# One more resident weight granule for one stream slot less, in a recurrent-memory attention kernel

## The chip, the cores and the metric

The kernel runs on one core of a Trainium2 chip. The metric is the device time of one execution in microseconds (us).

## The reference, cut to what matters

```python
for s in range(n_seg):                                   # 64 segments of 32 rows, one after the other
    h = jnp.concatenate([mem, xs], axis=1)               # 8 memory rows + 32 rows of the segment
    q, k, v = (einsum('btd,dhe->bhte', h, W) for W in (Wq, Wk, Wv))   # D=1024, 32 heads of 128
    p = softmax(mask(q @ k.T * scale))
    o = einsum('bhte,hed->btd', p @ v, Wo)
    mem = o[:, :M, :]                                    # the next segment needs this
    outs.append(o[:, M:, :])
# + a 2-token expert layer (w_gate, w_up, w_down) and two residual sums at the end
```

The memory rows make the segments sequential. Every segment needs all of Wq, Wk, Wv and Wo: 4 x 8 MB in bf16. That is 64 pieces of 512 KB, called granules, and they do not all fit beside each other in the core's memory.

Of the kernel before, what the change touches and what calls it, by code (L numbers as in the profile page):

```python
# [14 lines left out]
PSUM = bass.MemoryType.PSUM  # L15
DRAM = bass.MemoryType.DRAM

N_RES = 42
N_SLOT = 6

HELD = (18, 27, 36)
NEG = -30000.0

PHASES = [(0, 0), (1, 0), (0, 1), (1, 1), (2, 0), (2, 1)]
# [3 lines left out]
def kernel(  # L28
# [42 lines left out]
    NG = 64  # L71
    n_str = NG - N_RES
    streamed = set(((2 * i + 1) * NG) // (2 * n_str) for i in range(n_str))
    assert all(g in streamed and g < 48 for g in HELD)

    def granule_dram(g):
        if g < 48:
            p, kc = divmod(g, KC)
            mat, half = PHASES[p]
            return Wqkv[mat][kc * P:(kc + 1) * P, 2048 * half:2048 * (half + 1)]  # L80
        w = g - 48
        return Wo2[2 * w * P:(2 * w + 2) * P, :].rearrange("(hh e) d -> e hh d", hh=2)

    def granule_out(t, g):
        return t[:, :] if g < 48 else t.rearrange("p (hh d) -> p hh d", hh=2)
# [3 lines left out]
    dram = ctx.enter_context(tc.tile_pool(name="dram", bufs=1, space=DRAM))  # L89
    wstream = ctx.enter_context(tc.tile_pool(name="wstream", bufs=N_SLOT))  # L90
    one = ctx.enter_context(tc.tile_pool(name="one", bufs=1, reuse_waits="tile"))
# [117 lines left out]
    def fetch():  # L209

        while flow:
            what = flow.pop(0)
            if what[0] == "w" and what[1] not in streamed:
                g = what[1]
                pool = wres
                if g >= 48:
                    if late["pool"] is None:
                        pc.close()
                        late["pool"] = lc.enter_context(tc.tile_pool(name="wlate", bufs=1, reuse_waits="tile"))
                    pool = late["pool"]  # L220
                t = res_tiles[g] = pool.tile([P, 2048], BF16, name=f"wres{g}", tag=f"wres{g}")
                nc.sync.dma_start(out=granule_out(t, g), in_=granule_dram(g))
                continue
            t = wstream.tile([P, 2048], BF16, tag="g", name="g")
            if what[0] == "w" and what[1] in held:
                nc.sync.dma_start(out=t[:, 0:1024], in_=granule_dram(what[1])[:, 0:1024])
                nc.scalar.copy(out=t[:, 1024:2048], in_=held[what[1]][:, :].bitcast(BF16))  # L227
            elif what[0] == "w" and what[1] in wo_in:
                nc.sync.dma_start(out=t[:, :], in_=wo_d[what[1]][:, :])
            elif what[0] == "w":  # L230
                nc.sync.dma_start(out=granule_out(t, what[1]), in_=granule_dram(what[1]))
            elif what[0] == "gu":
                _, w, kc, fh = what
                nc.sync.dma_start(out=t[:, 0:FH], in_=(B_w_gate, B_w_up)[w][kc * P:(kc + 1) * P, FH * fh:FH * (fh + 1)])
            elif what[0] == "dn":
                nc.sync.dma_start(out=t.rearrange("p (a d) -> p a d", a=2),
                                  in_=B_w_down[2 * what[1] * P:(2 * what[1] + 2) * P, :].rearrange("(a p) d -> p a d", a=2))
            queued.append((what, t))
            return
# [6 lines left out]
    lc = ExitStack()  # L246
    for _ in range(N_SLOT):
        fetch()
# [93 lines left out]
    def used(g):  # L342
        if g in streamed:
            fetch()
# [65 lines left out]
    def left_pass(L, kc, Gv):  # L410

        for jq in range(4):
            nc.tensor.matmul(L["ps"][32 * jq:32 * jq + 32, :], lhsT=cur["stl"][:, kc, :],  # L413
                             rhs=Gv[:, 512 * jq:512 * (jq + 1)], start=(not L["had"]), stop=(len(L["had"]) == KC - 1),
                             tile_position=(0, 32 * jq))
        L["had"].append(kc)

    def left_bank():
        return {"ps": psL.tile([P, 512], F32, tag="accl", name="PSl"), "had": []}

    begun = {}
    for s in range(NSEG):
# [183 lines left out]
        for p, (mat, half) in enumerate(PHASES):  # L606
# [3 lines left out]
            lag, behind = 2 if j == 0 else 0, []  # L610
            for kc in range(KC):
                g = 8 * p + kc
                Gv = granule(g)
                for jq in range(4):
                    nc.tensor.matmul(PSm[32 * jq:32 * jq + 32, :], lhsT=ST[:, kc, :], rhs=Gv[:, 512 * jq:512 * (jq + 1)],  # L615
                                     start=(kc == 0), stop=(kc == KC - 1), tile_position=(0, 32 * jq))
                if s == 0 and g in HELD:
                    held[g] = psC.tile([P, 512], U32, tag=f"c{HELD.index(g)}", name="HELD")
                    nc.vector.tensor_scalar(out=held[g][:, :], in0=Gv[:, 1024:2048].bitcast(U32), scalar1=0, scalar2=None,
# [55 lines left out]
        n_wl, behind = 0, []  # L675

        def project_left(w, Gv, WL=WL if j == 3 else None, lhs=lhs_left):

            nonlocal n_wl
            for hs in range(2):  # L680
                for a in range(2):
                    q0 = 64 * hs + 32 * a
                    nc.tensor.matmul(WL[q0:q0 + 32, :], lhsT=lhs(2 * w + hs),  # L683
                                     rhs=Gv[:, D * hs + 512 * a:D * hs + 512 * (a + 1)], start=(n_wl == 0), stop=False,
                                     tile_position=(0, q0), skip_group_check=True)
            n_wl += 1
# [29 lines left out]
        nl = left_of(s + 1) if s + 1 < NSEG else {}  # L716
        if j == 3:
            fill = [lambda w=w, Gv=Gv: project_left(w, Gv) for w, Gv in behind[:4]]
            spots = [(0, 1), (0, 2), (0, 3), (0, 5), (0, 7), (1, 1)]
            todo += [(pk, lambda w=w, Gv=Gv, go=project_left: go(w, Gv)) for pk, (w, Gv) in zip(spots, behind[4:])]  # L720
            assert len(behind) == 10
        elif j == 1 or j == 2:
            for mat in nl:
                begun[mat] = left_bank()
                fill = [lambda kc=kc, g=8 * mat + kc, L=begun[mat]: left_pass(L, kc, res_tiles[g])
                        for kc in range(KC) if 8 * mat + kc not in streamed]
# [40 lines left out]
    for w in range(2):  # L767
        for fh in range(2):
            GU[w, fh] = psA.tile([P, 512], F32, tag="acc", name="GU") if w == 0 else \
                psC.tile([P, 512], F32, tag=f"c{fh}", name="GU")  # L770
        for kc in range(KC):
            for fh in range(2):
                Gt = take("gu", w, kc, fh)

                for q in range(4):
                    nb = 4 if q < 2 else 3
                    nc.tensor.matmul(GU[w, fh][32 * q:32 * q + 32, 0:nb * P], lhsT=XSP[:, kc, :],
                                     rhs=Gt.rearrange("p (b q c) -> p q b c", q=4, c=P)[:, q, 0:nb, :],
                                     start=(kc == 0), stop=(kc == KC - 1), tile_position=(0, 32 * q))
                fetch()  # L780
                n += 1
                if n in (6, 14):
                    todo[-2 + (6, 14).index(n)][1]()
# [71 lines left out]
```

## The kernel before: the parts that the change touches

42 granules stay resident; the other 22 are loaded again in each segment through a ring of six slots. A slot and a resident granule are the same size, and 42 + 6 = 48 of them are all that fits beside the kernel's other tiles. Three streamed granules are special: half of each is held in PSUM (the matrix engine's result memory), so that only the other 256 KB are loaded. These are the "held halves".

```python
N_RES = 42
N_SLOT = 6
HELD = (18, 27, 36)
...
n_str = NG - N_RES
streamed = set(((2 * i + 1) * NG) // (2 * n_str) for i in range(n_str))
...
wstream = ctx.enter_context(tc.tile_pool(name="wstream", bufs=N_SLOT))
...
t = wstream.tile([P, 2048], BF16, tag="g", name="g")     # waits for the slot to be released
if what[0] == "w" and what[1] in held:                    # half of it is kept in PSUM
    nc.sync.dma_start(out=t[:, 0:1024], in_=granule_dram(what[1])[:, 0:1024])
    nc.scalar.copy(out=t[:, 1024:2048], in_=held[what[1]][:, :].bitcast(BF16))
elif what[0] == "w" and what[1] in wo_in:                 # Wo copied once into contiguous scratch
    nc.sync.dma_start(out=t[:, :], in_=wo_d[what[1]][:, :])
elif what[0] == "w":
    nc.sync.dma_start(out=granule_out(t, what[1]), in_=granule_dram(what[1]))
...
lag, behind = 2 if j == 0 else 0, []                      # j = s % 4
for kc in range(KC):                                      # 6 phases of 8 granules: Q, K, Q, K, V, V
    Gv = granule(g)
    for jq in range(4):
        nc.tensor.matmul(PSm[32 * jq:32 * jq + 32, :], lhsT=ST[:, kc, :], rhs=Gv[:, 512 * jq:512 * (jq + 1)], ...)
    ...                                                   # some segments: a "left pass", the same granule once more
    used(g)                                               # issues the next load, which waits for a free slot
...
for w in range(16):                                       # output projection: granules 48 to 63
    project(WO, w, Gv, lhs_main, w == 15)
    used(48 + w)
```

Phases, the softmax and the projection differ a little by j = s % 4, the "remainder" below: the left passes (rows that four segments share) fall in remainders 2, 3 and 0, and the projection of those rows in remainder 3 and the start of 0.

## Time and profile before

| | before |
|---|---|
| median of all 36 runs, us | 2049 (medians of the five sets: 2046 to 2050) |
| bytes moved by DMA | 771.7 MB |
| mean period of segments 4 to 59 | 29.6 us |
| bytes a segment | 11.26 MB |

A segment's period is taken from one start of the transposes that put the memory rows into the stationary tile (L317 in the kernel before) to the next. The lines that the argument rests on are shown and read in the prediction. In these lines PE is the matrix engine (PEld its weight loads), DVE, ACT and POOL are the other engines, and SP issues the weight loads; tile g is a stream slot and tile wres a resident granule. Landing is the moment at which a load is known to have arrived; a slot's hold is the time from there to the next issue into it. Where a number below is called a tally, it was worked out from the trace's records of single packets, issues and landings, not printed by a view.

### The profile page before, as it was taken

Reading aid. Unit: us, or ns where it says so; the run is one execution under the profiler, and the core shown is the slowest. Engines: PE = TensorE matmul, PEld = TensorE weight load, DVE = VectorE, ACT = ScalarE, POOL = GpSimd, SP = SyncE. Lnnn points to the kernel's source line nnn. Section 1 sums busy time; section 2 is a strip of 40 time slices with the busy share of each in tenths; the row PEclk is TensorE's granted clock in tenths of the full one; section 3 lists DMA queues with packets and bytes.
Section 4 is the critical chain, followed back from the end, with each engine's and each line's share of the span. In section 5 each row is a group of like instructions: output and inputs, shape, how many; then the busy total and the mean of one; then the engine's idle time right before and its main releaser. Section 6 shows DMA issues by size and latency. Waiting matters only on the chain.

```text
span 2053.8 us, 80700 instructions
## 1 busy us (share of the span) xinstructions
PE 1723.0 (84%) x35178; PEld 863.7 (42%) x35178; DVE 760.2 (37%) x2360; ACT 717.9 (35%) x1754; POOL 525.5 (26%) x1004
## 2 busy tenths in 40 slices
PE   2578888888888888898988988898898888888776
PEld 1234444444444444444444444444444444444331
DVE  5523333333343333334333433343333333333420
ACT  3623333333333333333333333333333333333320
POOL 4422222222222222222231322223222222222110
PEclk8689999999999999999999999999999999999986
DMA  9999999999999999999999999999999999999998
GB/s 358 334 375 388 375 401 362 385 380 378 382 380 387 391 383 354 366 387 376 395 391 383 378 374 383 372 379 382 391 374 367 388 379 375 380 391 371 357 345 332
DMA packets 248230, 771.73 MB, mean 376 GB/s; under 512 B 37042, under 2 KB 42354, under 8 KB 247876
## 3 DMA queue, kind: packets, MB, share of 16 engines
q1 hardware_dynamic: 221188, 732.79, 93.8%
q0 software_dynamic: 23872, 29.19, 4.1%
q8 instruction: 275, 4.51, 0.8%
q10 hardware_dynamic: 2816, 4.59, 0.6%
q14 instruction: 79, 0.65, 0.1%
HBM read 753.82 MB, written 15.74 MB: 375 GB/s over the span
## 4 chain that ended last, share of the span: by engine, by line
DMA 56%; PE 35%; DVE 3%; ACT 2%; issue 2%; POOL 1%; ACTq 0%; DVEq 0%; SPq 0%; POOLq 0%
PE PSm L615 19%; DMA g<-wo_d 18%; DMA g<-in_A_Wv_dram 13%; DMA g<-in_A_Wq_dram 12%; PE PSl L413 5%; PE OA L664 3%; PE PTq L453 2%; DMA out_dram<-OB 2%; DMA g<-in_A_Wk_dram 2%; DMA g<-in_A_Wo_dram 1%; DMA QKL<-qkl_d 1%; PE WL L683 1%; DMA qkl_d<-QS 1%; DMA wres<-in_A_Wo_dram 1%; DMA g<-in_B_w_gate_dram 1%
## 5 line engine op out<-in xcount | busy, mean ns | idle before, releaser
L615 PE MATMUL PSm<-wres,ST 128*32 128x512 bf16 x8192 | 751.9, 392 | 5.7 <-DVE ST L318 5.1
L615 PE MATMUL PSm<-g,ST 128*32 128x512 bf16 x4096 | 419.0, 392 | 78.8 <-DMA g<-in_A_Wv_dram 38.5
L615 PEld LDWEIGHTS <-ST 128*32 128x32 bf16 x12288 | 300.0, 96 | 409.5 <-issue 175.2
L664 PEld LDWEIGHTS <-OT 128*32 128x32 bf16 x8192 | 218.0, 98 | 169.3 <-issue 146.7
L227 ACT COPY g<-HELD 128x1024 bf16<-128x1024 bf16 x189 | 191.4, 1013 | 199.2 <-PE PSm L615 117.3
L634 ACT CAST XB<-PSm 128x512 bf16<-128x512 f32 x256 | 149.9, 586 | 282.5 <-PE PSm L615 281.9
L664 PE MATMUL OA<-wres,OT 128*32 128x256 bf16 x5120 | 234.8, 280 | 14.1 <-issue 8.7
L664 PE MATMUL OA<-g,OT 128*32 128x256 bf16 x3072 | 160.2, 280 | 94.0 <-DMA g<-wo_d 79.7
L413 PE MATMUL PSl<-wres,STL 128*32 128x512 bf16 x2048 | 181.2, 389 | 13.8 <-DVE XBl L638 13.2
L561 ACT CAST OT<-OA 128x128 bf16<-128x128 f32 x256 | 67.9, 265 | 256.1 <-PE OP L555 254.1
L349 POOL DMA_DIRECT2D QKL<-qkl_d x126 | 91.8, 729 | 227.7 <-PE SPS L497 89.8
L710 POOL DMA_DIRECT2D out_dram<-OB x256 | 129.5, 513 | 54.2 <-DVE OB L706 33.7
L485 POOL COPY KT<-QKL 128x128 bf16<-128x128 bf16 x128 | 37.6, 293 | 403.4 <-PE OA L664 300.5
L561 DVE CAST OT<-OP 128x128 bf16<-128x128 f32 x128 | 37.3, 291 | 252.5 <-PE OP L555 252.5
L502 DVE TENSOR_REDUCE NM<-SPS 128x8 f32<-128x320 f32 x128 | 62.9, 491 | 170.2 <-PE SPS L497 170.2
L413 PEld LDWEIGHTS <-STL 128*32 128x32 bf16 x3072 | 83.4, 98 | 88.2 <-issue 36.4
L453 PE MATMUL PTq<-IDENT,XB 128*128 128x128 bf16 x1024 | 102.9, 224 | 20.2 <-ACT XB L634 18.8
L646 ACT CAST VM<-PSm 128x512 bf16<-128x512 f32 x128 | 77.4, 604 | 116.5 <-PE PSm L615 109.0
L413 PE MATMUL PSl<-g,STL 128*32 128x512 bf16 x1024 | 102.6, 388 | 11.5 <-DVE XBl L638 8.7
L453 PEld LDWEIGHTS <-XB 128*128 128x128 bf16 x1024 | 58.8, 98 | 124.6 <-ACT XB L634 69.2
L473 POOL DMA_DIRECT2D qkl_d<-QS x64 | 36.5, 570 | 275.5 <-ACT QS L469 259.7
L706 DVE CAST OB<-OA 128x128 bf16<-128x128 f32 x64 | 18.6, 291 | 228.5 <-ACT OB L705 175.8
(143 smaller groups left out, 2334.3 us busy)
## 6 DMA issues: line engine op xcount, KB each, us to landing
g<-wo_d SPq DMA_DIRECT2D x363, 512.0 KB, 7.1
g<-in_A_Wq_dram SPq DMA_DIRECT2D x321, 512.0 KB, 7.8
g<-in_A_Wk_dram SPq DMA_DIRECT2D x257, 512.0 KB, 6.6
g<-in_A_Wv_dram SPq DMA_DIRECT2D x257, 512.0 KB, 6.8
g<-in_A_Wq_dram SPq DMA_DIRECT2D x63, 256.0 KB, 5.7
g<-in_A_Wk_dram SPq DMA_DIRECT2D x63, 256.0 KB, 5.7
g<-in_A_Wv_dram SPq DMA_DIRECT2D x63, 256.0 KB, 6.5
g<-in_A_Wo_dram SPq DMA_DIRECT2D x21, 512.0 KB, 8.0
```

The costliest lines, as they stand in the source:

```text
L227: nc.scalar.copy(out=t[:, 1024:2048], in_=held[what[1]][:, :].bitcast(BF16))
L349: nc.gpsimd.dma_start(out=t[:, :, :], in_=qkl_d[s // 4][:, half, :, s % 4, :].rearrange("m p c -> p m c"))
L413: nc.tensor.matmul(L["ps"][32 * jq:32 * jq + 32, :], lhsT=cur["stl"][:, kc, :], rhs=Gv[:, 512 * jq:512 * (jq + 1)], start=(not L["had"]), ...
L453: nc.tensor.transpose(out=PTq[:, il, :, :].rearrange("p j r -> p (j r)"), in_=XB[:, il * P:(il + 1) * P], identity=IDENT[:, :])
L485: nc.gpsimd.tensor_copy(out=keys(half)[:, :, 32:NK], in_=QKL[half][:, 1, :].rearrange("p (h r) -> p h r", r=XL))
L502: nc.vector.tensor_reduce(out=NM[:, :], in_=S8, axis=AX.X, op=ALU.max, negate=True)
L561: copy(out=OT[half][:, 2 * ph + jl, :, :], in_=ov[:, :, 0:SEG])
L615: nc.tensor.matmul(PSm[32 * jq:32 * jq + 32, :], lhsT=ST[:, kc, :], rhs=Gv[:, 512 * jq:512 * (jq + 1)], start=(kc == 0), stop=(kc == KC - ...
L634: nc.scalar.copy(out=XB[:, :], in_=PSm[:, :])
L646: nc.scalar.copy(out=VM[half][:, :], in_=PSm[:, :])
L664: nc.tensor.matmul(PS[32 * g:32 * g + 32, 0:256], lhsT=lhs(h), rhs=Gv[:, D * hs + 256 * g:D * hs + 256 * (g + 1)], start=(first and hs == ...
L710: nc.gpsimd.dma_start(out=out2[s * SEG:s * SEG + XM, 256 * g:256 * (g + 1)], in_=OB[32 * g:32 * g + XM, 0:256])
```

## The change

Keep 43 granules and stream 21, with five slots; the held halves move to other granules of the new streamed set. The intent: earlier changes let slots go sooner, so five might be enough, and the freed slot saves 0.52 MB in each of 63 segments.

```diff
-N_RES = 42
-N_SLOT = 6
+N_RES = 43
+N_SLOT = 5
 
-HELD = (18, 27, 36)
+HELD = (19, 25, 32)
@@ in fetch()
-                if g >= 48:
+                if g >= 49:
@@ the left rows' projection: one more resident granule to defer
-            spots = [(0, 1), (0, 2), (0, 3), (0, 5), (0, 7), (1, 1)]
+            spots = [(0, 1), (0, 2), (0, 3), (0, 5), (0, 6), (0, 7), (1, 1)]
...
-            assert len(behind) == 10
```

## The prediction

> **What bounds the kernel now.** I read the page first: the busy shares, the slices and the chain that ended last.
>
> ```profile
> PE 1723.0 (84%) x35178; PEld 863.7 (42%) x35178; DVE 760.2 (37%) x2360; ACT 717.9 (35%) x1754; POOL 525.5 (26%) x1004
> DMA  9999999999999999999999999999999999999998
> GB/s 358 334 375 388 375 401 362 385 380 378 382 380 387 391 383 354 366 387 376 395 391 383 378 374 383 372 379 382 391 374 367 388 379 375 380 391 371 357 345 332
> DMA packets 248230, 771.73 MB, mean 376 GB/s; under 512 B 37042, under 2 KB 42354, under 8 KB 247876
> DMA 56%; PE 35%; DVE 3%; ACT 2%; issue 2%; POOL 1%; ACTq 0%; DVEq 0%; SPq 0%; POOLq 0%
> ```
>
> The DMA engines are at nine tenths or more in 39 of 40 slices, and 56% of the chain is DMA. So the kernel looks bound by the weight stream. But PE is at 84%, and 35% of the chain is PE: the second limit is near. Next I cut the steady part into segments (a segment begins where PE transposes the memory rows into the stationary tile, L317) and read the windows of four successive segments, number 28 to 31, that is remainder 0, 1, 2, 3 of the group of four. Columns: window, then PE, PEld, DVE, ACT, POOL busy, granted clock, DMA share, GB/s.
>
> ```profile
> 922.04:951.96 29.92, 26.47 (x582) 13.82 (x580) 11.40 (x38) 11.12 (x28) 7.33 (x15) 1.00 1.00 368
> 951.96:981.84 29.88, 24.31 (x489) 11.69 (x490) 10.92 (x36) 9.49 (x24) 8.02 (x17) 1.00 1.01 389
> 981.84:1010.85 29.01, 25.89 (x554) 13.20 (x552) 10.62 (x33) 10.82 (x27) 6.50 (x14) 1.00 1.01 392
> 1010.85:1039.32 28.47, 26.41 (x571) 14.08 (x568) 11.12 (x34) 10.66 (x26) 9.04 (x19) 1.00 1.02 400
> ```
>
> A segment takes 28.5 to 29.9 us, and 63 of them (114.6 to 1990 us, roughly) are nearly the whole span; the mean of segments 4 to 59 is 29.6 us. The third view is who PE waits for between 500 and 1500 us (us in total, times, longest):
>
> ```profile
> PE OA L664 <- DMA g<-wo_d: 39.1, 76, 1.9
> PE PSm L615 <- DMA g<-in_A_Wv_dram: 15.7, 26, 1.6
> PE PSm L615 <- DMA g<-in_A_Wq_dram: 15.1, 33, 1.4
> PE PTq L453 <- ACT XB L634: 10.8, 17, 2.7
> PE OA L664 <- issue: 6.3, 8, 1.8
> PE PSm L615 <- DMA g<-in_A_Wk_dram: 4.9, 14, 0.7
> ```
>
> Waits for streamed granules are 39.1 + 15.7 + 15.1 + 4.9 = 75 us of 1000, 7.5%. That is 2.2 us of a 29.6 us segment. **If the stream were free, a segment would still take about 29.6 - 2.2 = 27.4 us.** Summed by remainder over segments 4 to 59, with the short waits that the view drops, the period less those waits is 28.7, 25.3, 26.9 and 27.5 us (mean 27.1). In remainder 0, PE and the work around it set the pace and the memory system falls to 368 GB/s; in remainder 1, the stream sets it. The last view is the stream itself: the issues, and for tile g the time to landing from 500 to 1500 us.
>
> ```profile
> g<-wo_d SPq DMA_DIRECT2D x363, 512.0 KB, 7.1
> g<-in_A_Wq_dram SPq DMA_DIRECT2D x321, 512.0 KB, 7.8
> g<-in_A_Wq_dram SPq DMA_DIRECT2D x63, 256.0 KB, 5.7
> DMA to landing us min/median/max: 4.2/6.8/10.0
> ```
>
> 22 loads a segment are one per 29.6/22 = 1.35 us, and with six slots one slot's cycle is 6 x 1.35 = 8.1 us: about 7.0 us from issue to landing, 1.1 us from landing to reissue (median by load 1.0 us; 1.5 in remainder 0, 0.7 in remainder 1).
>
> **What the Trainium skill says.** "DMA: Bandwidth & Descriptors", section Specifications, gives a fabric ceiling of 435 GB/s and about 358 GB/s of HBM per core; this trace holds 380 over long stretches and 401 in one slice, so the second is not the limit here, and there is room above 380. The same page, Anatomy of one DMA, splits a DMA into a fixed part of about 2 us, mostly completion latency, and bytes/436e9: for 512 KB an estimate of 2.0 + 1.2 = 3.2 us. The fit is for the software path, these loads use the hardware one; the shortest landing above is 4.2 us. Both say that a slot spends a good part of its cycle not moving bytes, so the number of slots buys rate. "Perfetto Trace Analysis", Optimization Strategy, says that a repeating gap on the engine that should be saturated can mean too few buffers; the dip in remainder 0 fits.
>
> **The change, part by part.** *One more resident granule.* 63 segments load 21 instead of 22: 63 x 0.524 = 33.0 MB less. The bytes of a segment (packet records, segments 4 to 59) are 11.26 MB, and become 10.74. At an unchanged 380 GB/s that is 0.524/0.380 = 1.38 us a segment, 87 us in all (28.2 us a segment). *Output projection.* Streamed granules of Wo go from six (48, 50, 53, 56, 59, 62) to five, so one copy into scratch memory (0.52 MB read, 0.52 written) falls away once: 1.05/0.380 = 2.8 us. *PE work* is the same 70,358 rows; one resident granule's left projection moves into the next segment (four matmuls, some 0.22 us, at a new spot), no more and no less work. *Held halves* sit at 19, 25, 32 instead of 18, 27, 36: still three half loads of 256 KB and three ACT copies of 1.0 us. *SBUF* is the same 48 granules. *One slot less.* This is the price. At 28.2 us a segment a slot's cycle would be 5 x 28.2/21 = 6.7 us; less 1.1 us of hold leaves 5.6 us from issue to landing, where 6.8 to 7.0 are used now and 4.2 is the least ever seen. The queue that keeps the engines fed shrinks from about 2.7 us to 1.4 us.
>
> What that does to the rate I took from a tally of the packet records before: bytes issued and not yet moved, microsecond by microsecond, against GB/s in the same microsecond and two later. With 3.0 to 3.5 granules outstanding it is 390 and 397, with 2.5 to 3.0 378 and 380, with 2.0 to 2.5 375 and 365, with 1.5 to 2.0 365 and 340, with 1.0 to 1.5 352 and 301. The mean is 2.9 now. A cycle 1.3 us shorter takes about one granule from it: 2.0 (estimate). I choose 368 GB/s there, above the middle of the two readings (370 and 352), because many thin moments of the old trace come when PE is late, which is also why the rate sinks after them. So 10.74/0.368 = 29.2 us a segment, 0.4 less than 29.6: **63 x 0.4 = 25 us**. With the copy, -28 us. The first segment and the expert layer at the end (46 loads through the same slots, already at 332 to 345 GB/s) pay for the thinner queue without saving bytes: +2 us by estimate. Sum -26: 2046.8 - 26 = about 2020 us.
>
> **Rivals.** *Full gain:* the rate stays at 380 and all 87 us come, 1960 us. For it: the stream's limit looks hard, and remainder 1 to 3 hold 389 to 400. Against it: remainder 0 is already at its 28.7 us without stream waits, so it can't reach 28.2. *PE becomes the bound:* each remainder takes the longer of its stream-free time and its stream time; with 0.52 MB less at 385 GB/s the latter are 26.7, 28.7, 28.5, 27.7, so 28.7 + 28.7 + 28.5 + 27.7 = 113.6, 28.4 a segment; with some loss where the two alternate, 28.7 and -57 us: 1990 us. It speaks for this that the stream-free times are only 4% under the stream's. *The slot was worth as much as the granule:* the lagged reading, 352 to 360 GB/s, gives 29.8 to 30.5 us a segment, nothing gained up to 2100 us. For it: in remainder 0 slots are held longest (1.5 us), where two left passes lag; against it: PE waits in the rest already release a slot at once (0.5 us at the least).
>
> **Range and chances.** The centre is 2020; the PE-bound rival is the low end, 1990; no gain is the high end, 2045. Faster by over 2% needs under 2006.7 us, a gain of 0.64 us a segment, which asks for 371 GB/s or better all through with a queue of half the length: 0.27. Slower by over 2% needs over 2087.8 us, which asks for under 354 GB/s: 0.03. The rest, 0.70, is within 2%.
>
> **What would show it.** Right: some 738 MB instead of 771.7; the median landing of g falling from 6.8 to some 5.5 us; mean rate from 376 to about 365 GB/s; PE waiting for g about as much as now, 60 to 80 us of the 1000, for a segment near 29.2 us. The full-gain rival shows 376 GB/s or more kept. The PE rival shows waits for g nearly gone and all segments within 27 to 29 us. The third shows waits for g above 80 us and a rate under 360. The prediction is wrong if the thin queue costs no rate (the tally mistook PE's lateness for the cause), or if the five slots hold back remainder 0 far more than the old trace shows.

## The result

The changed kernel took **2121.5 us** (median, 2118.2 to 2135.3), the kernel before 2045.8 us in the same set. The ratio is **1.038**, 95% interval 1.033 to 1.043: slower. Ratios here are the mean time of one kernel's fast runs over that of the other's of the same rounds, so not quite the ratio of the medians.

The page of the changed kernel: busy shares, the DMA and bandwidth slices, the packets, and the engines of the chain that ended last.

```profile
PE 1719.9 (81%) x35178; PEld 871.5 (41%) x35178; DVE 761.9 (36%) x2360; ACT 718.5 (34%) x1754; POOL 526.4 (25%) x1003
DMA  9899999999999999999999999999999999999998
GB/s 358 322 367 365 339 354 355 357 346 353 361 348 363 327 359 340 343 354 344 342 355 356 352 343 349 329 368 355 361 345 360 353 351 344 344 351 342 333 329 333
DMA packets 238373, 738.16 MB, mean 349 GB/s; under 512 B 36018, under 2 KB 41330, under 8 KB 238020
DMA 58%; PE 34%; ACT 3%; DVE 2%; issue 2%; POOL 1%; SPq 0%; ACTq 0%; DVEq 0%; POOLq 0%
```

The bytes fell by 33.6 MB, as intended. The rate fell with them, from 376 to 349 GB/s over the span, and by more than the bytes. The row of DMA digits is as full as before, and the chain has nearly the same shares: neither shows the loss. Only the GB/s row does.

The windows of segments 28 to 31 of the changed kernel (columns as in the prediction: window, PE, PEld, DVE, ACT, POOL busy, granted clock, DMA share, GB/s):

```profile
946.84:978.20 31.36, 26.86 (x586) 14.06 (x583) 11.38 (x38) 11.12 (x28) 7.33 (x15) 1.00 0.96 334
978.20:1008.62 30.42, 23.99 (x490) 12.18 (x490) 10.94 (x36) 9.60 (x24) 8.06 (x17) 0.94 0.99 355
1008.62:1040.03 31.41, 26.33 (x552) 13.45 (x551) 10.62 (x33) 11.07 (x27) 6.51 (x13) 1.00 0.98 356
1040.03:1070.95 30.92, 26.66 (x567) 13.88 (x564) 11.13 (x34) 10.68 (x26) 8.46 (x17) 1.00 0.97 345
```

All four are longer by 0.5 to 2.5 us, and each runs at 334 to 356 GB/s where it ran at 368 to 400. PE's waits from 500 to 1500 us (total us, times, longest):

```profile
PE OA L664 <- DMA g<-wo_d: 53.9, 94, 2.0
PE PSm L615 <- DMA g<-in_A_Wv_dram: 31.7, 53, 2.8
PE PSm L615 <- DMA g<-in_A_Wq_dram: 19.1, 31, 1.5
PE PSm L615 <- DMA g<-in_A_Wk_dram: 9.3, 15, 1.8
```

Waits for granules are 114 us of the 1000, before 75. So the time lies in PE waiting for a slower stream. The issues (KB, median us to landing), and tile g's landing from 500 to 1500 us:

```profile
g<-in_A_Wq_dram SPq DMA_DIRECT2D x321, 512.0 KB, 6.3
g<-in_A_Wv_dram SPq DMA_DIRECT2D x321, 512.0 KB, 6.3
g<-wo_d SPq DMA_DIRECT2D x305, 512.0 KB, 6.8
DMA to landing us min/median/max: 3.7/6.2/8.5
```

A load still takes 6.2 us to land, where 5.5 to 5.6 had been predicted. The mean period of segments 4 to 59 is 30.63 us for 10.73 MB.

### The profile page after: what moved, and what is told of

It reads as the page before. It is cut to its first block, busy times and chain, and to the rows that moved or that the text cites. A ratio compares the mean times of both kernels' runs of the same rounds, so it can differ in the third digit from the quotient of the medians.

```text
span 2116.3 us, 80574 instructions
## 1 busy us (share of the span) xinstructions
PE 1719.9 (81%) x35178; PEld 871.5 (41%) x35178; DVE 761.9 (36%) x2360; ACT 718.5 (34%) x1754; POOL 526.4 (25%) x1003
## 2 busy tenths in 40 slices
DMA packets 238373, 738.16 MB, mean 349 GB/s; under 512 B 36018, under 2 KB 41330, under 8 KB 238020
## 4 chain that ended last, share of the span: by engine, by line
DMA 58%; PE 34%; ACT 3%; DVE 2%; issue 2%; POOL 1%; SPq 0%; ACTq 0%; DVEq 0%; POOLq 0%
DMA g<-wo_d 18%; DMA g<-in_A_Wv_dram 18%; PE PSm L615 17%; DMA g<-in_A_Wq_dram 12%; PE PSl L413 6%; DMA g<-in_A_Wk_dram 4%; PE OA L664 3%; PE PTq L453 2%; PE WL L683 1%; DMA wres<-in_A_Wo_dram 1%; DMA g<-in_B_w_up_dram 1%; DMA g<-in_A_Wo_dram 1%; DMA g<-in_B_w_gate_dram 1%; PE SPS L497 1%; PE PTm L317 1%
## 5 line engine op out<-in xcount | busy, mean ns | idle before, releaser
L615 PE MATMUL PSm<-wres,ST 128*32 128x512 bf16 x8192 | 717.6, 392 | 6.4 <-DVE ST L318 5.1
L615 PEld LDWEIGHTS <-ST 128*32 128x32 bf16 x12288 | 311.6, 97 | 460.1 <-issue 218.0
L664 PE MATMUL OA<-wres,OT 128*32 128x256 bf16 x5632 | 249.1, 281 | 15.0 <-issue 7.7
L664 PE MATMUL OA<-g,OT 128*32 128x256 bf16 x2560 | 133.2, 282 | 102.3 <-DMA g<-wo_d 92.3
L413 PE MATMUL PSl<-wres,STL 128*32 128x512 bf16 x2048 | 186.2, 393 | 11.6 <-DVE XBl L638 7.5
```

The lines of the kernel that those rows point to most:

```text
L413: nc.tensor.matmul(L["ps"][32 * jq:32 * jq + 32, :], lhsT=cur["stl"][:, kc, :], rhs=Gv[:, 512 * jq:512 * (jq + 1)], start=(not L["had"]), ...
L664: nc.tensor.matmul(PS[32 * g:32 * g + 32, 0:256], lhsT=lhs(h), rhs=Gv[:, D * hs + 256 * g:D * hs + 256 * (g + 1)], start=(first and hs == ...
```

## The experiments

Theory A: a load passes through a cycle of which much is not transfer, so five slots can't carry more than some 350 GB/s, whatever they carry. Theory B: the new places of the held halves thin the stream. A further question was what the granule is worth if the slot is not given up. Each kernel ran three rounds against the kernel before, one of them five. Where the memory does not hold the wanted sizes, one or more resident granules share another's tile. This gives wrong values (the comparison with the reference passed all the same) and saves those loads once, in the first segment.

| kernel | resident / slots | held halves | median us | ratio to before | GB/s, 500 to 1500 us |
|---|---|---|---|---|---|
| before | 42 / 6 | 18, 27, 36 | 2046 to 2050, by set | 1 | 381 |
| changed | 43 / 5 | 19, 25, 32 | 2121 | 1.038 | 350 |
| r42s5 | 42 / 5 | as before | 2202 | 1.075 | 354 |
| r43s5old | 43 / 5 | 19, 28, 35 | 2135 | 1.043 | 351 |
| r43s5spread | 43 / 5 | 10, 25, 41 | 2139 | 1.044 | 350 |
| r43s5lag0 | 43 / 5, lag 0 | 19, 25, 32 | 2120 | 1.032 | 354 |
| r43s6w | 43 / 6 | 19, 25, 32 | 2039 | 0.994 | 366 |
| r43s6old | 43 / 6 | 19, 28, 35 | 2012 | 0.982 | 371 |
| r43s8w | 43 / 8 | 19, 25, 32 | 1986 | 0.967 | 370 |
| r42s7w | 42 / 7 | as before | 2020 | 0.985 | 386 |
| r42s6near | 42 / 6 | 18, 24, 30 | 2078 | 1.014 | 372 |
| r42s6wide | 42 / 6 | 18, 30, 42 | 2056 | 1.004 | 380 |
| r42s6lag0 | 42 / 6, lag 0 | as before | 2050 | 0.999 | 381 |
| nostream | 42 / none from segment 1 | - | 1759 | 0.857 | 19 |

### The slot alone: r42s5

```diff
 N_RES = 42
-N_SLOT = 6
+N_SLOT = 5
```

> 42 resident granules, five slots, held halves where the kernel before has them: the slot taken away alone. Theory A (the slot pays for the rate: with five slots the loads run at some 350 GB/s, with six at 380): 11.26 MB a segment at 350 GB/s is 32.2 us, 63 x 2.6 = 160 us slower than before, some 2200 us. Theory B (what hurts is the new places of the held halves, 19, 25 and 32, which stand at every second load and leave few bytes in flight): old places, so little loss, under 2090 us.

2202 us, ratio 1.075 (1.069 to 1.081), as theory A had it. The window from 500 to 1500 us, of the kernel before, of the changed one and of this one:

```profile
500.00:1500.00 1000.00, 882.12 (x18521) 449.96 (x18514) 370.30 (x1164) 355.94 (x884) 253.91 (x505) 0.98 1.00 381
```

```profile
500.00:1500.00 1000.00, 846.29 (x17849) 436.95 (x17845) 359.17 (x1130) 341.31 (x857) 247.21 (x488) 0.98 0.97 350
```

```profile
500.00:1500.00 1000.00, 841.32 (x17127) 420.31 (x17123) 345.50 (x1084) 326.71 (x821) 240.56 (x478) 0.97 0.98 354
```

The last column falls from 381 to 350 and 354. The column before it, the DMA share, stays between 0.97 and 1.00. The granted clock, one column further left, is 0.97 to 0.98 in all three, so the clock is no rival. The period is 31.82 us for 11.27 MB. So the slot costs some 155 us alone (2048 in the same set), and with five slots the granule is then worth 2202 - 2121 = 81 us, nearly the 87 that the prediction gave it (67 us if the changed kernel has its halves at 19, 28, 35: 2202 - 2135, r43s5old below).

### The granule alone: r43s6w, r43s6old

```diff
 N_RES = 43
-N_SLOT = 5
+N_SLOT = 6
+SAME = {63: 61}
@@ in fetch(), for resident granules
+                if g in SAME:
+                    res_tiles[g] = res_tiles[SAME[g]]
+                    continue
```

> 43 resident granules and six slots, which do not fit in memory; granule 63 shares granule 61's tile, so the result is wrong on purpose and one load less is done once. The granule taken away alone, with the held halves at the new places. Theory A: the rate stays near 380 GB/s, 10.73 MB a segment in 28.3 to 28.9 us, some 1960 to 2000 us. Theory B (the new places are the cause): no better than before, 2040 us or more.

2039 us, 0.994 (0.989 to 0.998). Theory A expected 1960 to 2000, and that missed: 33 MB less gave 8 us. PE's longest waits from 500 to 1500 us:

```profile
PE OA L668 <- DMA g<-wo_d: 29.0, 57, 1.8
PE PTq L457 <- ACT XB L638: 27.2, 48, 2.8
PE OA L668 <- issue: 20.1, 21, 2.3
```

All its waits for granules are 42 us of the 1000, where the kernel before had 75: the stream did come closer. But other waits grew, the two last lines from 10.8 and 6.3 us. What they are is taken up under "More slots". r43s6old is the same kernel with HELD = (19, 28, 35):

> 43 resident granules and six slots (granule 63 shares 61's tile, values wrong on purpose) with the held halves at 19, 28 and 35, three loads apart as in the kernel before, instead of 19, 25 and 32. If the close places are why the granule alone was worth only 8 us: 1990 to 2020 us. If PE's side is the limit: within 0.7% of that run, 2025 to 2050 us.

2012 us, 0.982 (0.977 to 0.987). The places of the halves do count here, 27 us, so theory B is right at six slots. The granule is worth 38 us at the better places (2050 in the same set), still far from 87. One correction to the expectations of this run and of r43s5old: with 43 resident granules 19, 28 and 35 are the loads 6, 9 and 11 of the 21, so they stand three and two loads apart, not three and three. The spacing of the kernel before was not tried with 43.

### The places of the held halves with five slots: r43s5spread, r43s5old

The changed kernel with HELD = (10, 25, 41), and with (19, 28, 35).

> The changed kernel with the held halves at 10, 25 and 41, five loads apart, so that never two of them are in five slots. Theory A: within 1% of the changed kernel, 2100 to 2140 us. Theory B: most of the loss comes back, 2060 us or less.

> The changed kernel with the held halves at 19, 28 and 35, three loads apart as before, instead of 19, 25 and 32: the third part of the change taken back. If the close places cost with five slots what they cost with six (27 us of 2039), 2090 to 2100 us, and the slot is then worth less than it seemed. If with five slots the queue is thin wherever the halves stand, within 0.7% of the changed kernel, 2107 to 2137 us.

2139 us (1.044) and 2135 us (1.043): no better than the changed kernel's 1.038 (the intervals overlap), at the same 350 and 351 GB/s. Theory B falls for the change itself: of the three sets of places tried with five slots none beats its new ones, though with six slots they cost 27 us.

### The places alone with six slots: r42s6near, r42s6wide

The kernel before with HELD = (18, 24, 30), and with (18, 30, 42).

> The kernel before with the held halves two loads apart, at 18, 24 and 30, instead of 18, 27 and 36: the places alone. If close places cost by themselves, 2070 to 2080 us (27 us as at 43 with six slots); if not, within 0.5% of before.

> The kernel before with the held halves four loads apart, at 18, 30 and 42, instead of three. A try at a version that beats both kernels. With six slots, going from two loads apart to three was worth 30 us with 42 resident granules and 27 us with 43. If distance itself is what counts (fewer half-filled slots at one time), some 5 to 15 us more, 2030 to 2043 us. If the places count for something else (which stretch of the segment they relieve), as likely slower, 2050 to 2080 us.

2078 us, 1.014 (1.012 to 1.017): two loads apart costs 30 us, as expected. But 2056 us, 1.004 (1.000 to 1.007) for four apart: distance is not all, and this try at something better than the kernel before failed. Why a place is good was not found.

### Does a lagging left pass hold up the slots: r43s5lag0, r42s6lag0

```diff
-            lag, behind = 2 if j == 0 else 0, []
+            lag, behind = 0, []
```

> The changed kernel with the left passes of remainder 0 right behind their granules (lag 0 for 2), so that they hold no slot two granules longer. If held slots are what thins the queue there, remainder 0 falls from 31.7 to some 30.5 us, 16 x 1.2 = 20 us, 2100 us. If the number of slots and the fixed part of a load do it, within 0.5% of the changed kernel.

> The kernel before without the lag of two granules for the left passes of remainder 0, the one place where a left pass still holds a slot longer. With five slots it moved nothing (2119.6 for 2121.5). If it is as idle with six, within 0.5% of before; if a held slot matters where the queue is deep enough to fill, 2030 us or less.

2120 us (1.032, 1.028 to 1.037) beside the changed kernel's 2121, and 2050 us (0.999, 0.996 to 1.003). With five slots the tally shows the hold in remainder 0 fall from 1.32 to 1.04 us and its period from 31.7 to 30.9 us, but the periods of remainders 1 and 2 rose by 0.4 us each (remainder 3 fell by 0.5; the mean is 30.5 for 30.6). The medians show no gain. (Its ratio looks better than its median because the kernel before was a little slower on that chip.)

### More slots: r42s7w, r43s8w

Seven slots with granule 63 in 61's tile and the late pool starting at granule 52; eight slots with 49, 51, 52, 54 and 55 in 48's tile and the late pool starting at 57.

> 42 resident granules and seven slots; granule 63 shares granule 61's tile (values wrong on purpose). The slot given instead of taken. If the rate goes on rising with slots, as from five to six (354 to 380 GB/s), it reaches some 400 GB/s: 28.2 us a segment, 1960 us. If the eight-slot run showed a limit on PE's side of 29.0 us that holds for any stream, a segment takes 29.0 to 29.3 us, 2005 to 2030 us: the sixth slot was worth 155 us, the seventh under 40.

> 43 resident granules and eight slots; granules 49, 51, 52, 54, 55 share granule 48's tile (wrong result on purpose, five loads less in the first segment, worth some 7 us). Theory A and the PE limit of the prediction: PE's waits for granules nearly vanish and a segment takes 27.1 to 28.4 us, 1900 to 1975 us in all. If instead the loads have their own ceiling near 380 GB/s, no better than six slots with 43 granules beyond those 7 us.

r42s7w: 2020 us, 0.985 (0.978 to 0.991). The sixth slot is worth 155 us, the seventh 30 (2050 in the same set):

```profile
500.00:1500.00 1000.00, 869.53 (x18786) 450.17 (x18782) 377.14 (x1186) 354.92 (x901) 260.53 (x518) 0.99 1.01 386
```

r43s8w: 1986 us, 0.967 (0.962 to 0.973), of which some 7 us are the five loads left out. Its period is 29.04 us. PE's longest waits from 500 to 1500 us (its lines stand four further down: L668 is the output projection, L298 and L457 are transposes), and a piece of its timeline:

```profile
PE OA L668 <- issue: 39.8, 28, 3.2
PE PTx L298 <- DVE KT L464: 23.1, 8, 4.2
PE PTq L457 <- ACT XB L638: 16.0, 40, 1.0
...
PE OA L668 <- DMA g<-wo_d: 0.3, 1, 0.3
```

```profile
506.88 0.39 PE L668 MATMUL OA<-g,OT 128*32 128x256 bf16 x8
509.96 0.40 PE L668 MATMUL OA<-wres,OT 128*32 128x256 bf16 x8 [2.69 <-issue]
```

With eight slots PE waits for streamed granules no more: 0.3 us in 1000. And yet a segment takes 29.0 us, only 0.6 less than before. Other waits took their place, first of all "issue", where PE stands still with nothing to wait for in the profile, here 2.7 us in the middle of a projection that reads resident weights. A tally of PE's standstills of 0.8 us or more with no releaser, from 150 to 1950 us: 7 in the kernel before (7.3 us), 23 in r43s6w (32 us) and in r42s7w (32 us), 49 in r43s8w (87 us). All 102 of them ended 1.2 to 1.7 us after a 16 KB packet of the instruction queue (q8 in the page) had finished; these packets come about every 7 us. "Runtime: NRT & Kernel Launch", Instruction fetch mechanics, says that a refill block is 16 KiB or 256 instructions; 275 packets of 16 KB on that queue make 70,400, and the page lists 2 x 35,178 = 70,356 matmuls and weight loads of PE. So I read this as PE waiting for its own instructions. The packet itself takes no longer than without the stream (median 0.96 us in r43s8w, 1.09 us in nostream below), so the delay would lie before it starts, which the trace does not show.

### No stream at all: nostream

From segment 1 on a streamed granule is read from the resident tile below it, and no load is issued.

```diff
-    flow += [("w", g) for s in range(1, NSEG) for g in sorted(streamed)]
-    at = len(flow) - 2 * n_str
-    flow[at:at] = [("work",)]
+    flow += [("work",)]
@@ granule(g)
-        return take("w", g) if g in streamed else res_tiles[g]
+        if g in streamed and s == 0:
+            return take("w", g)
+        while g in streamed:
+            g -= 1
+        return res_tiles[g]
@@ used(g)
-        if g in streamed:
+        if g in streamed and s == 0:
```

> The kernel before, but from the second segment on a streamed granule is read from the resident tile below it, so no weights are loaded there (wrong values on purpose); PE's instructions are the same. Measures what PE's side takes by itself. The prediction's subtraction of waits says 27.1 us a segment, about 1890 us in all. If PE's side has its own limit of 29.0 us: about 2005 us. If the stream's traffic is what delays PE's instruction fetches and the small loads: 25 to 26.5 us a segment, 1760 to 1850 us.

1759 us, 0.857 (0.854 to 0.861). The window from 500 to 1500 us, then PE's longest waits in it:

```profile
500.00:1500.00 1000.00, 964.84 (x21806) 513.23 (x21802) 435.88 (x1375) 300.46 (x927) 302.12 (x599) 1.00 0.07 19
```

```profile
PE PTq L455 <- ACT XB L636: 9.4, 20, 0.7
PE PTq L455 <- DVE SC L266: 6.8, 10, 0.7
PE PTm L315 <- ACT OB L707: 4.5, 11, 0.4
PE PTx L292 <- DVE KT L462: 2.0, 10, 0.2
```

A segment takes 25.1 us, PE is 96% busy, the tally finds none of those standstills, and the waits of up to 4.2 us behind the small loads' chain (L298 above, L292 here) are down to 0.2 us. The small loads themselves land sooner: tile QKL after a median of 2.4 us instead of 6.0 in r43s8w, tile XL after 2.0 instead of 6.0. So the stream costs PE time also where PE waits for no granule. That it does so by delaying other transfers is measured for these small loads, and rests on the timing alone for the 87 us of instruction waits; what each adds to the time of a segment is not taken apart. The three ACT copies a segment are gone too in this run, so it is not the stream alone that was removed.

## Why the prediction was wrong, point by point

**Right:** the bytes (738 MB predicted, 738.16 measured; 10.74 and 10.73 MB a segment), the hold of a slot (1.1 and 1.08 us), and the value of the granule with five slots (87, and 67 to 81 us by the places of the halves). The direction of the price was seen too, and the third rival, in which the slot is worth as much as the granule, is what happened, somewhat beyond its 2100 us: its signs were a rate under 360 GB/s and waits above 80 us, and the run shows 349 and 114.

**The step that failed: "I choose 368 GB/s there".** The measured rate of the steady part is 350, and all five kernels with five slots lie at 350 to 354, whatever their bytes, places and lag. The prediction had two readings of its tally at 2.0 granules, 370 and, two microseconds later, 352; it leaned to the first, and the second is what came. 10.73 MB at 350 GB/s is 30.66 us instead of 29.19: 1.47 x 63 = 93 us, which puts the prediction of 2020 at 2113, close to the 2121 measured. So the mechanism was there and its size was off: the slot's price was put at 58 us (10.74/0.368 against 10.74/0.380, times 63), and it is some 155 us with 42 residents, 2135 - 2012 = 123 us with 43 and the halves at 19, 28, 35, and 2121 - 2039 = 82 us with 43 at the change's own places. The parts do not simply add, since with six slots other waits keep back most of what the granule saves: its 8 us there less the 82 make the same loss of 74 us as 81 less 155.

**The sign named last, remainder 0.** Its mean period rose most, from 29.8 to 31.7 us, that is by nearly half of what the four lost together (remainder 1 stayed at 30.0, 2 rose from 30.0 to 30.8, 3 from 28.7 to 30.1). The lag is not why the whole is slower: without it remainder 0 recovers 0.8 us and the total does not.

**Why the tally misled.** It took the state of the stream to be the bytes issued and not yet moved. That mean fell from 2.9 to 2.3 granules, not even as far as the 2.0 predicted, and the rate fell further all the same. With 2.0 to 2.5 granules outstanding the kernel before moved 375 GB/s, the changed one 355. Tallied parts of one load's cycle, in us:

| | issue to first bytes | moving | last bytes to landing | hold | sum |
|---|---|---|---|---|---|
| before | 3.76 | 1.50 | 1.68 | 1.17 | 8.1 |
| changed | 3.09 | 1.62 | 1.50 | 1.08 | 7.3 |

The first part is 1.9 us even at its 5th percentile. I take this as the time for which an issued load is under way before it can move, and outstanding bytes include such loads. The figure is rough: a second tally, with packets given to loads in order of start, has 1.8 to 2.3 us there and 1.0 us for the quickest load. Counting a load only from 1.9 us after its issue, the mean is 1.8 granules before and 1.3 after, and the share of moments with less than one is 14% before, 36% after, 33% in r42s5 and 11% in r42s7w (11, 31, 27 and 9% in the second tally: the same order). By this reading the cycle could not shrink to the 6.7 us of the plan since only about 1.9 us of it was queue: it gave up 0.8 us, and the rate paid for the rest. No run tests this part by itself. The packets show the loss though no DMA engine looks idle: a 4096-byte packet of the stream has a median of 159 ns in both kernels, but the mean rises from 169.5 to 179.5 ns and the 95th percentile from 192 to 269 ns. Why a packet takes longer when little is queued is not visible in the trace and stays open.

**The other wrong step: "If the stream were free, a segment would still take about 27.4 us".** Subtracting waits does not give what is left without their cause. With almost no granule waits left (r43s8w) a segment takes 29.0 us; waits marked "issue" and waits behind small loads stand where the granule waits stood. With no stream at all it takes 25.1 us. So the "full gain" and "PE becomes the bound" rivals were mis-sized as well: with the slot kept, the granule gives 8 to 38 us, not 57 to 87.

**The reading that began it.** DMA digits of nine were taken as a full stream. The share is 0.96 to 1.02 at anything from 334 to 400 GB/s. "Perfetto Trace Analysis", Identifying the Most-Contended Engine, warns of this: it advises against occupancy for DMA because of the 16 engines, and for bandwidth.

No run that fits in memory beat the kernel before. All that did have their values spoilt; the smallest step, 43/6 or 42/7, needs 4 KB a partition that are not there.

## What to carry to other kernels

Price a prefetch slot by the load's whole cycle, from issue to the next issue, and by how much of that cycle is not queue; here one slot of six took 7 to 8% of the rate (381 to 350 or 354 GB/s), though DMA still looked busy. Read GB/s, not the busy share, to see whether a stream is at its ceiling. And do not take "period less waits" for the time that is left without their cause: measure it, with a run in which the loads are left out.

## What the Trainium skill lacked or had wrong

- "Runtime: NRT & Kernel Launch", Instruction fetch mechanics, says that fetching is hidden because instructions are issued more slowly than they come. Under a full weight stream the timing speaks against it: 49 standstills of PE of 0.9 to 3.6 us, 87 us in all, in r43s8w, each ending 1.2 to 1.7 us after a 16 KB instruction packet; none without the stream. That a block is 16 KB for 256 instructions agrees.
- "DMA: Bandwidth & Descriptors", Anatomy of one DMA, gives a fit for the software path only (an estimate of 3.2 us for 512 KB). On the hardware path here the stream's loads took 6.2 to 6.8 us (medians) under load, of which by tally 3.1 to 3.8 us passed before the first bytes and 1.5 to 1.7 us between the last bytes and the landing.
- No page that I read says how the rate depends on the number of loads in flight. For 512 KB loads here: 350 to 354 GB/s with five slots; with 42 residents 381 with six and 386 with seven; with 43 residents, where PE waits less for granules, 366 to 371 with six and 370 with eight.
